# Attention and two expert layers on one core: half splits begun later, one weight chunk in four of the first layer whole, logits on strips, a new border

## The chip, the cores and the metric

One core of a Trainium2 chip runs the whole program. Its engines work side by side, each in its own fixed order, and meet by semaphores: TensorE (PE; its weight loads are listed apart as PEld), VectorE (DVE), ScalarE (ACT), GpSimd (POOL) and SyncE (SP, which here only issues DMAs). The metric is the device time of one execution in microseconds (us).

## The reference

Causal linear attention with a decay per head, then two layers of experts with top-1 routing, in float32:

```python
for t in range(768):                         # 2 batches, 8 heads of 64
    state = gamma * state + outer(k[t], v[t])
    y[t] = (q[t] @ state) / 8
x = y as 1536 tokens x 512
# layer A: tokens with x @ w_skip > 0, 8 experts, hidden size 1024
e = argmax(x @ w_gate); g = softmax weight of e
x = x + g * (relu(x @ w1[e]) @ w2[e])        # the other tokens stay as they are
# layer B: every token, other weights, at most 384 tokens for an expert
out = g' * (relu(x @ w1'[e']) @ w2'[e'])
```

Each layer has 8 experts of 2 x 512 x 1024 weights: 32 chunks of 128 x 2048 float32 (1 MB), so 64 chunks in all.

## The kernel before

**Attention** goes over 6 chunks of 128 positions with 2 batches each (`attention`). For a chunk, `scores` multiplies q and k, `state` adds k·v into the running state (k is first scaled by the decays on POOL, `scale_k`), `outs` forms the output. The kernel is written as generators; after each `yield` one step of the side work is taken (`step_side`), and the order so written is each engine's order. Side work of a chunk is `sink` in `route_tokens`: router logits, choice of the expert (`pick`, some seven small DVE operations), the token's rank among its expert's tokens (`ranked`), its place as a row of ones and zeros (`where`), and `to_slots`, which adds the token's number into a table of slots on PE. Rows go to a table in DRAM, from which each expert's 128 tokens are gathered. The **border** is the last chunk's sink: the first expert's tokens are put together on PE without the table (`place`).

**Layer A** takes the experts in turn: `layer1` (24 matmuls of 512 columns), a transposed hidden block (`split_T`), and one expert later `layer2` (24 matmuls). A float32 product is made of three fast ones (`mm3`): each weight chunk is split into a high part `hi` (ACT copy, L197) and a low part `lo` (DVE subtraction, L198), activations likewise. After each part of such work a *turn* takes place: one step of the routing into layer B (`route_b`: row, transposes, logits, choice, rank, `whereb`, `to_slots`) and, every second turn, `pump`, which splits one whole chunk and issues one load. Raw chunks land in 3 tiles during attention and 4 afterwards, split chunks live in 4 and then 6 pairs of tiles. An expert has 11 turns: four in `layer1`, one for the next x, four in `layer2`, two for the hidden block's transposes.

**Layer B** runs expert 0's first half on 128 tokens, then the other half, then the experts 1 to 7 on 256 tokens each (`pair_layer1`, `pair_layer2`, 8 turns for an expert).

At the start POOL's order holds all constants (`constants`, L132 to L148), which wait for a DMA of constants, and then the first `scale_k`. SP issues the loads of chunk 1 ahead of the DMA of those constants.

Of the kernel before, what the change touches and what calls it, by code (L numbers as in the profile page):

```python
# [26 lines left out]
NRAW, NRAW2 = 3, 1  # L27
NW, NW2 = 4, 2
# [12 lines left out]
def kernel(  # L41
# [54 lines left out]
    row2 = [const.tile([128, RW], F32, name=f"row2{i}") for i in range(3)]  # L96
# [6 lines left out]

    mask = const.tile([128, 2, 4, 128], F32, name="mask")
    row0 = const.tile([128, 2, 128], F32, name="row0")
    gq = cs[:, C_GQ:C_GQ + 512].rearrange("p (r t) -> p r t", r=4)
    rev = cs[:, C_REV:C_REV + 8]
    zsum = const.tile([128, 8], F32, name="zsum")
# [17 lines left out]
    def constants():  # L126
# [3 lines left out]
        nc.sync.dma_start(out=table[0:1, :], in_=zb[0:1, :].bitcast(F32))  # L130
        for t in t9.values():
            nc.gpsimd.memset(t, 0.5)  # L132
        nc.gpsimd.memset(cum, 0.0)
        nc.gpsimd.memset(cumb, 2.0)
        for t in row2:
            nc.gpsimd.memset(t[:, DM:RW], 0.0)
# [7 lines left out]
        nc.gpsimd.tensor_tensor(out=zsum, in0=ident[:, 8:16], in1=ident[:, 40:48], op=ALU.add)  # L144
        for i in (72, 104):
            nc.gpsimd.tensor_tensor(out=zsum, in0=zsum, in1=ident[:, i:i + 8], op=ALU.add)
# [10 lines left out]
    def add_chunks(ap, e, kind):  # L157
        for j in range(2):
            order.append(((kind, e, j), ap[e, j]))
# [11 lines left out]
    raw_free, w_free = [raw_p] * NRAW, [w_p] * NW  # L171
    count = {"load": 0, "split": 0}
    held = {}

    def load_w():
        i = count["load"]
        if i < len(order) and raw_free:
            count["load"] += 1
            pool = raw_free.pop(0)
            t = pool.tile([128, 2048], F32, tag="raw", name="raw")  # L180
            nc.sync.dma_start(out=t, in_=order[i][1])
            raw_t[i] = (t, pool)

    def split_w(n=1):

        i = count["split"]
        count["split"] += 1
        key = order[i][0]
        pool = w_free.pop(0)
# [3 lines left out]
        raw, raw_pool = raw_t.pop(i)  # L193
        r3 = raw.rearrange("p (k f) -> p k f", k=4)
        parts = [slice(4 * j // n, 4 * (j + 1) // n) for j in range(n)]
        for j, k in enumerate(parts):
# [16 lines left out]
    def first_splits():  # L213
        while w_free and count["split"] < len(order):
            while count["split"] >= count["load"]:
                yield
            yield from split_w(4)
            yield
            load_w()
# [100 lines left out]
    def route_tokens(rows, rows_p):  # L320

        late, acc, xhl, m_of = [], [], [], {}

        def sink(c, xt, bs, psum):
            rc = rows[c % len(rows)]
            end = c == NCH - 1
            n = len(bs)
            b0, b1 = bs[0], bs[-1] + 1
            lt = psum("s", 4)
            for i, b in enumerate(bs):  # L330
                for k in range(KT):
                    nc.tensor.matmul(
                        out=lt[:, 32 * i:32 * i + 18], lhsT=xt[:, b, k, :], rhs=wgt[:, k, 0:18],
                        start=k == 0, stop=k == KT - 1, skip_group_check=True,
                    )
            nc.gpsimd.tensor_copy(out=rc[:, b0:b1, IDCOL:IDCOL + 1], in_=tok[:, b0:b1, c:c + 1])
            yield
            lg = lt[:, 0:32 * n].rearrange("p (a c) -> p a c", a=n)
            m, gate = pick(lg, n, 2, None, rc[:, b0:b1, GCOL:GCOL + 2])
            m3 = m.rearrange("p (a g) j -> p a (g j)", a=n)  # L340
            m2d = m.rearrange("p n j -> p (n j)")
            rhs = sm.tile([128, n, 2, 16], BF16, tag=f"rhs{n}", name="rhs")
            eng = nc.vector if end else nc.gpsimd
            if not end:
                gate()
            if end and not acc:
                acc.extend([psum("m"), psum("m")])
                place(acc, a0, ident, True, False)
                for w in late[0:2]:
                    place(acc, *w, False, False)  # L350
            yield
            xrs = []

            def rows_T(b):
                xr = psum("s", 4)
                for k in range(KT):
                    nc.tensor.transpose(xr[:, 128 * k:128 * k + 128], xt[:, b, k, :], ident)
                nc.scalar.activation(out=rc[:, b, 0:DM], in_=xr, func=ACTF.Copy)

            def rank():  # L360
                rk = psum("s", 4)
                ranked(rk, lc[:, 0, :], m2d, cum[:, 0:n, :].rearrange("p a j -> p (a j)"), [m_of[0]] if end and b0 else [])
                pr = sm.tile([128, n, 16], F32, tag=f"pr{n}", name="pr")
                sl = sm.tile([128, n], F32, tag=f"sl{n}", name="sl")
                rk3 = rk[:, 0:16 * n].rearrange("p (a j) -> p a j", a=n)
                nc.vector.tensor_tensor(out=pr, in0=rk3, in1=m3, op=ALU.mult)
# [22 lines left out]
            if not end:  # L389
                for b in bs:  # L390
                    rows_T(b)
                    yield
# [729 lines left out]
```

## Time and profile before

| | |
|---|---|
| median of 3 runs | 488.28 us (485.61 to 489.3) |
| the profiled execution's own time | 484.47 us |
| its span (first to last instruction) | 482.7 us |
| PE busy | 407.8 us, 84% of the span |
| PEld, DVE, ACT, POOL busy | 71%, 53%, 43%, 28% |
| mean granted clock of TensorE | 0.927 of 2.4 GHz |
| moved by DMA | 96.24 MB, 199 GB/s over the span |

The share of busy time is a mean over stages with different limits, so the stages are read apart: attention with its border (to 102.45 us), layer A's expert 0 (to 109.86), its experts 1 to 7 (to 259.74), the passage to layer B with the last product of A and the first of B (to 298.32), and layer B. A row names line, engine, operation, written tile <- read tiles, shape and count; a matmul's own time runs to its modelled end, so how fast matmuls follow each other is read from two starts. A plain float32 matmul stands as two instructions in the trace.

### The profile page before, as it was taken

Reading aid. Unit: us, or ns where it says so; the run is one execution under the profiler, and the core shown is the slowest. Engines: PE = TensorE matmul, PEld = TensorE weight load, DVE = VectorE, ACT = ScalarE, POOL = GpSimd, SP = SyncE. Lnnn points to the kernel's source line nnn. Section 1 sums busy time; section 2 is a strip of 40 time slices with the busy share of each in tenths; the row PEclk is TensorE's granted clock in tenths of the full one; section 3 lists DMA queues with packets and bytes.
Section 4 is the critical chain, followed back from the end, with each engine's and each line's share of the span. In section 5 each row is a group of like instructions: output and inputs, shape, how many; then the busy total and the mean of one; then the engine's idle time right before and its main releaser. Section 6 shows DMA issues by size and latency. Waiting matters only on the chain. (4 is left out here: it accounts for less than half of the span.)

```text
span 482.7 us, 6907 instructions
## 1 busy us (share of the span) xinstructions
PE 407.8 (84%) x2734; PEld 342.6 (71%) x2734; DVE 253.8 (53%) x404; ACT 209.5 (43%) x260; POOL 135.3 (28%) x188
## 2 busy tenths in 40 slices
PE   7498888978488776967776779899999999999994
PEld 3377777967456564755555557798989898989993
DVE  4055854559646746655585341675546464646110
ACT  0235523158463553744362320755555454545111
POOL 2456744158020403121013105011413132232201
PEclk9599989899888997979796889999999999999999
DMA  8477894159945847474756344385857575631100
GB/s 329 168 303 292 321 338 168 45 200 328 366 175 195 310 170 236 179 261 134 238 188 234 109 154 134 100 286 178 281 177 276 177 258 182 239 125 45 43 1 33
DMA packets 17979, 96.24 MB, mean 199 GB/s; under 512 B 2447, under 2 KB 2575, under 8 KB 8340
## 3 DMA queue, kind: packets, MB, share of 16 engines
q1 hardware_dynamic: 11636, 80.06, 47.2%
q0 software_dynamic: 3360, 10.02, 6.0%
q10 hardware_dynamic: 2944, 5.65, 3.2%
q8 instruction: 23, 0.38, 0.3%
q14 instruction: 16, 0.13, 0.1%
HBM read 87.29 MB, written 9.48 MB: 200 GB/s over the span
## 5 line engine op out<-in xcount | busy, mean ns | idle before, releaser
L198 DVE TENSOR_TENSOR lo<-raw,hi 128x2048 fp32r<-128x2048 f32 (+1 forms) x76 | 149.8, 1980 | 109.3 <-ACT hi L197 109.3
L197 ACT ACTIVATE hi<-raw 128x2048 fp32r<-128x2048 f32 (+1 forms) x76 | 123.6, 1640 | 40.3 <-issue 19.8
L641 PE MATMUL o<-hi,hTh 128*128 128x512 f32 x192 | 84.0, 438 | 1.4 <-ACT hTh L313 1.4
L643 PE MATMUL o<-hi,hTl 128*128 128x512 f32 x192 | 81.0, 422 | 2.4 <-DVE hTl L314 2.4
L642 PE MATMUL o<-lo,hTh 128*128 128x512 f32 x192 | 80.5, 419 | 0.0
L641 PE MATMUL s<-xh,hi 128*128 128x256 f32 x224 | 63.7, 284 | 0.0
L643 PE MATMUL s<-xh,lo 128*128 128x256 f32 x224 | 63.4, 283 | 0.0
L642 PE MATMUL s<-xl,hi 128*128 128x256 f32 x224 | 63.4, 283 | 0.0
L749 POOL DMA_INDIRECT out_dram<-y,ixo x16 | 18.1, 1131 | 135.0 <-ACT y L746 103.2
L643 PEld LDWEIGHTS o<-hi,hTl 128*128 128x128 f32 x192 | 39.5, 206 | 12.3 <-DVE hTl L314 3.2
L641 PEld LDWEIGHTS o<-hi,hTh 128*128 128x128 f32 x192 | 39.2, 204 | 9.0 <-ACT hTh L313 1.6
L642 PEld LDWEIGHTS o<-lo,hTh 128*128 128x128 f32 x192 | 39.6, 206 | 7.3
L641 PEld LDWEIGHTS s<-xh,hi 128*128 128x128 f32 x224 | 42.9, 192 | 0.3
L642 PEld LDWEIGHTS s<-xl,hi 128*128 128x128 f32 x224 | 42.9, 192 | 0.3
L643 PEld LDWEIGHTS s<-xh,lo 128*128 128x128 f32 x224 | 42.9, 192 | 0.0
L641 PE MATMUL s<-hi,xh 128*128 128x512 f32 x80 | 35.6, 445 | 1.9 <-DVE xl L314 0.9
L716 POOL TENSOR_SCALAR rhsb<-m,cs 128x8 bf16<-128x8 bf16 x8 | 2.5, 309 | 123.0 <-DVE se L255 123.0
L887 ACT ACTIVATE hTh<-s 128x512 fp32r<-128x512 f32 x28 | 16.8, 599 | 41.6 <-PE s L643 41.6
L888 DVE SCALAR_TENSOR_TENSOR hTl<-s,hTh 128x512 fp32r<-128x512 f32 x28 | 19.3, 689 | 28.3 <-ACT hTh L887 28.3
L643 PE MATMUL s<-hi,xl 128*128 128x512 f32 x80 | 32.4, 406 | 0.9 <-DVE xl L314 0.9
L642 PE MATMUL s<-lo,xh 128*128 128x512 f32 x80 | 32.5, 406 | 0.0
L515 DVE TENSOR_TENSOR p<-s,mask 128x512 f32<-128x512 f32 x24 | 15.4, 685 | 26.9 <-PE s L506 26.9
(155 smaller groups left out, 566.5 us busy)
## 6 DMA issues: line engine op xcount, KB each, us to landing
raw<-in_w1a_dram SPq DMA_DIRECT2D x16, 1024.0 KB, 5.6
raw<-in_w2a_dram SPq DMA_DIRECT2D x16, 1024.0 KB, 6.8
raw<-in_w1b_dram SPq DMA_DIRECT2D x16, 1024.0 KB, 5.1
raw<-in_w2b_dram SPq DMA_DIRECT2D x16, 1024.0 KB, 5.0
kv<-in_qkv_dram SPq DMA_DIRECT2D x6, 1024.0 KB, 9.9
qk<-in_qkv_dram SPq DMA_DIRECT2D x5, 1024.0 KB, 7.7
table<-rowc ACTq DMA_DIRECT2D x5, 516.0 KB, 4.1
table<-row ACTq DMA_DIRECT2D x8, 258.0 KB, 3.3
```

The lines of the kernel that those rows point to most:

```text
L197: nc.scalar.activation(out=hi[:, k], in_=r3[:, k], func=ACTF.Copy)
L198: nc.vector.tensor_tensor(out=lo[:, k], in0=r3[:, k], in1=hi[:, k].bitcast(F32), op=ALU.subtract)
L515: nc.vector.tensor_tensor(out=t.rearrange("p r t -> p (r t)"), in0=sa[j], in1=mask[:, j].rearrange("p r t -> p (r t)"), op=ALU.mult)
L641: nc.tensor.matmul(out=acc, lhsT=a[0], rhs=w[0], start=first, stop=False)
L642: nc.tensor.matmul(out=acc, lhsT=a[0], rhs=w[1], start=False, stop=False)
L643: nc.tensor.matmul(out=acc, lhsT=a[1], rhs=w[0], start=False, stop=last)
L716: nc.gpsimd.tensor_scalar(out=rhs[:, 0, :], in0=m, scalar1=p1, scalar2=None, op0=ALU.mult)
L749: new = nc.gpsimd.indirect_dma_start(out=out[:, :], out_offset=bass.IndirectOffsetOnAxis(ap=ix, axis=0), in_=y, in_offset=None, bounds_che ...
L887: nc.scalar.activation(out=hi[:, g:g + 2, :], in_=acc, func=ACTF.Relu)
L888: nc.vector.scalar_tensor_tensor(out=lo[:, g:g + 2, :], in0=acc, scalar=0.0, in1=hi[:, g:g + 2, :].bitcast(F32), op0=ALU.max, op1=ALU.subtract
```

## The change

- **Splits in halves.** `pump` runs at every turn and issues half a chunk's split (n = 2; in attention still a quarter, n = 4, from chunk 2 on). A chunk may be split only four turns after its load was issued (`LANDING`), and a pair of tiles is given out only two turns after its last use. Raw tiles are 3 and then 5, pairs 4 and then 5. In layer B's experts 1 to 7 a turn issues two halves.
- **Whole chunks.** The second `w2a` chunk of each of the 8 experts of layer A is not split: `layer2` multiplies it as float32 out of its raw tile, against a hidden half that is only copied.
- **Logits on strips.** In attention the four partial products of the router stand in four strips of 32 columns and are added up by a second matmul after an ACT copy, where 48 matmuls with 18 columns stood.
- **Border and start.** `to_slots` of the chunks comes a step later; the last chunk's sink is written out by itself; the small DMAs of constants are issued ahead of chunk 1's loads and the constants are worked out after the first `scale_k`. `route_b` puts one more turn between `whereb` and `to_slots`.

```diff
-NRAW, NRAW2 = 3, 1
-NW, NW2 = 4, 2
+LANDING = 4
+NRAW, NRAW2 = 3, 2
+NW, NW2 = 4, 1
...
+    def whole(kind, j):
+        return kind == "w2a" and j == 1
...
     def load_w():
-        i = count["load"]
-        if i < len(order) and raw_free:
+        while count["load"] < len(order) and raw_free:
+            i = count["load"]
...
+            key, _, divided = order[i]
+            if divided:
+                raw_t[i] = (t, pool, count["turn"])
+            else:
+                wt[key], held[key] = t.rearrange("p (k f) -> p k f", k=4), pool
+
+    def next_split():
+        while count["split"] < len(order) and not order[count["split"]][2]:
+            count["split"] += 1
+        i = count["split"]
+        if i in raw_t and w_free and w_free[0][0] <= count["turn"] and raw_t[i][2] + LANDING <= count["turn"]:
+            return i
...
     def used(key):
-        w_free.append(held.pop(key))
-
-    def pump():
-        if w_free and count["split"] < count["load"]:
-            for _ in split_w():
-                pass
-        load_w()
+        pool = held.pop(key)
+        if key in whole_keys:
+            raw_free.append(pool)
+        else:
+            w_free.append((count["turn"] + 2, pool))
...
+    def pump(n, pieces):
+        count["turn"] += 1
+        for _ in range(pieces):
+            if not splitting:
+                i = next_split()
+                if i is None:
+                    break
+                splitting.append(split_w(i, n))
+            try:
+                next(splitting[0])
+            except StopIteration:
+                splitting.clear()
+        load_w()
...
+        def logits(xt, bs, psum):
+            n = len(bs)
+            ls = psum("s", 4)
+            for k in range(KT):
+                nc.tensor.matmul(
+                    out=ls[32 * k:32 * k + 32, 0:128 * n], lhsT=wgt[:, k, :], rhs=xt[:, bs[0]:bs[-1] + 1, k, :], start=True, stop=True
+                )
+            lgs = sm.tile([128, 256], F32, tag="lgs", name="lgs")
+            nc.scalar.activation(out=lgs[:, 0:128 * n], in_=ls[:, 0:128 * n], func=ACTF.Copy)
+            return lgs
+
+        def summed(lgs, n, psum):
+            lt = psum("s", 4)
+            for i in range(n):
+                nc.tensor.matmul(
+                    out=lt[:, 32 * i:32 * i + 18], lhsT=lgs[:, 128 * i:128 * i + 128], rhs=zsum[:, 0:18], start=True, stop=True
+                )
+            return lt[:, 0:32 * n].rearrange("p (a c) -> p a c", a=n)
...
+        def last_chunk(xt, psum):
...
+            lg[0] = logits(xt, [0], psum)
+            yield
+            picked(0)
+            rows_T(xt, rc, 0, psum)
+            yield
+            lg[1] = logits(xt, [1], psum)
+            warm(psum("m"), 2)
+            picked(1)
+            placed(0)
+            rows_T(xt, rc, 1, psum)
+            acc = [psum("m"), psum("m")]
+            place(acc, a0, ident, True, False)
+            placed(1)
+            to_slots(where[0], rhs[0][:, 0], 0, 16)
+            place(acc, *late[0], False, False)
+            for b in range(B):
+                gates[b]()
+                write_rows(nc.scalar, rc[:, b:b + 1, :], 1)
...
+            for g in range(2):
+                ks = slice(2 * g, 2 * g + 2)
+                place(acc, *late[1], False, True, range(KT)[ks])
+                split(acc[g][:, 0:256].rearrange("p (k t) -> p k t", k=2), hi[:, ks], lo[:, ks])
...
-                    if c + 1 < NCH:
-                        load(c + 1)
-                    if pump and c == 0:
-                        constants()
...
+                if pump and c == 0:
+                    constants()
+                if c + 1 < NCH:
+                    load(c + 1)
+                if pump and c:
+                    load_w()
+                if c < NCH - 1:
+                    scale_k(c)
+                if pump and c == 0:
+                    derived()
...
     def layer2(hT, kind, e):
...
+            if whole(kind, k // 4):
+                nc.tensor.matmul(out=acc, lhsT=a[0][:, k % 4, :], rhs=w[:, k % 4, :], start=k == 0, stop=k == FT - 1)
+            else:
+                mm3(acc, at_k(a, k % 4), at_k(w, k % 4), k == 0, k == FT - 1)
...
             late.append((r2, oh))
-        yield
+        yield from idle(2)
         to_slots(where, rhs, 8, 8)
...
-        turns[0] += 1
-        if turns[0] % 2:
-            pump()
+        pump(2, pieces[0])
```

The order moves most on POOL at the start. Before, from the first constant that reads the DMA of constants (`cs`) to the second chunk's `scale_k`:

```order
L138 MEMSET rowc_103 128x2x4
L139 ISA
L139 TENSOR_SCALAR his<-cs 128x12
L141 TENSOR_SCALAR iota<-cs 128x128 x2
L144 TENSOR_TENSOR zsum<-cs 128x8
L146 TENSOR_TENSOR zsum<-zsum,cs 128x8 x2
L147 CAST lc<-cs 128x256
L148 CAST cap<-cap_i 1x1
L483 TENSOR_TENSOR kv<-kv,cs 128x512 x2
L497 TENSOR_TENSOR gqc<-cs 128x512
```

And in the changed program, on POOL from the row mask on:

```order
L516 MEMSET row_133 1x128 x2
L549 ISA
L549 TENSOR_TENSOR kv<-kv,cs 128x512 x2
L132 MEMSET t_108 128x9
L132 MEMSET t_109 128x18
...
L137 TENSOR_SCALAR his<-cs 128x12
L139 TENSOR_SCALAR iota<-cs 128x128 x2
L142 TENSOR_TENSOR zsum<-cs 128x32
L144 TENSOR_TENSOR zsum<-zsum,cs 128x32 x2
L145 CAST lc<-cs 128x256
L146 CAST cap<-cap_i 1x1
L563 TENSOR_TENSOR gqc<-cs 128x512
```

The scaling of k (`kv`) now stands ahead of everything that reads the second DMA of constants.

DVE in one expert of layer A before, from the end of the choice (`RECIPROCAL`) to the next hidden block (`lo` is a weight split, `xl` the next x, `prb` to `whereb` the rank, `row` the token rows, `hTl` the hidden block):

```order
L258 RECIPROCAL row_97<-sf 128x1
L198 TENSOR_TENSOR lo<-raw,hi 128x2048
L314 TENSOR_TENSOR xl<-t,xh 128x512
L198 TENSOR_TENSOR lo<-raw,hi 128x2048
L722 TENSOR_TENSOR prb<-t,m 128x8
L724 TENSOR_REDUCE slb<-prb 128x1
L726 TENSOR_SCALAR whereb<-iota,slb 128x256
L198 TENSOR_TENSOR lo<-raw,hi 128x2048 x2
L686 SCALAR_TENSOR_TENSOR row_98<-o,rowc_103 128x512
L314 TENSOR_TENSOR hTl<-t,hTh 128x512 x2
```

The same stretch of DVE in the changed program:

```order
L279 RECIPROCAL row_1213<-sf 128x1
L212 TENSOR_TENSOR lo<-raw,hi 128x1024 x2
L335 TENSOR_TENSOR xl<-t,xh 128x512
L212 TENSOR_TENSOR lo<-raw,hi 128x1024
L802 TENSOR_TENSOR prb<-t,m 128x8
L804 TENSOR_REDUCE slb<-prb 128x1
L806 TENSOR_SCALAR whereb<-iota,slb 128x256
L212 TENSOR_TENSOR lo<-raw,hi 128x1024 x3
L766 SCALAR_TENSOR_TENSOR row_1214<-o,rowc_100 128x512
L335 TENSOR_TENSOR hTl<-t,hTh 128x4x128
```

Three halves stand ahead of the rank where two whole splits stood, three more halves ahead of `row` where two whole ones stood, and one of the two `hTl` is gone.

PE around `to_slots` (L278, L299) in the same expert, changed program (`hTw` is the hidden half that is only copied):

```order
L717 MATMUL o<-lo,hTh 128x512
L718 MATMUL o<-hi,hTl 128x512
L743 MATMUL o<-raw,hTw 128x512 x2
L299 LDWEIGHTS whereb
L299 MATMUL tab<-rhsb,whereb 128x8
...
L299 LDWEIGHTS whereb
L299 MATMUL tab<-rhsb,whereb 128x8
L743 MATMUL o<-raw,hTw 128x512 x2
L699 MATMUL t<-cs,h 128x128 x8
```

Before, six fast matmuls stood between the rank's matmuls and `to_slots`; now these six and two plain float32 ones do.

## Rows read from the trace of the kernel before

**Rows 1.** Windows: span, PE, PEld, DVE, ACT, POOL busy; clock, DMA share, GB/s.
```profile
109.86:259.74 149.88, 115.00 (x540) 87.12 (x540) 94.31 (x125) 77.05 (x82) 34.71 (x47) 0.86 0.67 235
259.74:298.32 38.58, 28.37 (x148) 21.48 (x147) 15.32 (x37) 10.43 (x17) 7.53 (x15) 0.87 0.39 128
298.32:476.50 178.18, 175.96 (x1120) 159.70 (x1120) 89.08 (x80) 84.28 (x88) 39.76 (x41) 1.00 0.49 164
151.59:161.86 10.27, 10.27 (x59) 7.71 (x57) 7.21 (x14) 8.27 (x11) 2.85 (x4) 1.00 0.53 186
```
**Rows 2.** Waits: who waited for whom, us in total, times, longest.
```profile
PE tab L278 <- DVE whereb L726: 21.6, 6, 3.8
PE t L700 <- DVE row L686: 16.4, 4, 6.1
PE u L528 <- POOL kv L483: 8.3, 1, 8.3
PE tab L278 <- DVE where L380: 7.2, 6, 2.5
```
**Rows 3.** Timeline, POOL and PE: start, us, operation, idle before.
```profile
15.41 0.33 POOL L139 TENSOR_SCALAR his<-cs 128x12 f32<-128x12 f32 x1 [11.50 <-DMA cs<-in_cst_dram]
17.94 2.03 POOL L483 TENSOR_TENSOR kv<-kv,cs 128x512 f32<-128x512 f32 x2
22.79 1.49 PE L506 MATMUL s<-qk 64*128 64x128 f32 x16
```
**Rows 4.** Window of the start, columns as in 1.
```profile
5.20:5.70 0.50, 0.50 (x3) 0.16 (x2) 0.00 (x0) 0.00 (x0) 0.00 (x0) 1.00 1.08 422
```
**Rows 5.** Timeline of PE: a chunk's logits; strips in layer A.
```profile
38.35 1.96 PE L332 MATMUL s<-wgt,xt 128*128 128x18 f32 x16
154.99 0.43 PE L706 MATMUL t<-x2t,wgt 128*32 128x128 f32 x8
155.34 0.50 PE L641 MATMUL s<-hi,xh 128*128 128x512 f32 x1
156.86 0.28 PE L711 MATMUL t<-zsum,lgsb 128*128 128x8 f32 x2
```
**Rows 6.** Window of the border, columns as in 1.
```profile
88.81:102.45 13.64, 10.14 (x87) 9.65 (x86) 7.46 (x41) 2.91 (x7) 0.87 (x1) 0.87 0.18 68
```
**Rows 7.** Timeline of DVE, border: a choice's first and last step.
```profile
90.75 0.17 DVE L238 TENSOR_REDUCE mx<-s 128x2 f32<-128x16 f32 x1 [0.66 <-PE s L332]
91.73 0.18 DVE L251 TENSOR_TENSOR m<-t,tm 128x16 bf16<-128x16 f32 x1
```
**Rows 8.** Timeline of DVE, layer A: the rank and the place.
```profile
164.66 0.15 DVE L722 TENSOR_TENSOR prb<-t,m 128x8 f32<-128x8 f32 x1
165.04 0.35 DVE L726 TENSOR_SCALAR whereb<-iota,slb 128x256 bf16<-128x256 f32 x1
```
**Rows 9.** Groups by line: busy us, mean ns of one, idle before.
```profile
L198 DVE TENSOR_TENSOR lo<-raw,hi 128x2048 fp32r<-128x2048 f32 x60 | 137.3, 2291 | 103.7 <-ACT hi L197 103.7
L198 DVE TENSOR_TENSOR lo<-raw,hi 128x512 fp32r<-128x512 f32 x16 | 12.5, 813 | 5.6 <-ACT hi L197 5.6
L314 DVE TENSOR_TENSOR xl<-t,xh 128x512 fp32r<-128x512 f32 x23 | 15.1, 684 | 7.4 <-issue 7.4
L686 DVE SCALAR_TENSOR_TENSOR row<-o,rowc 128x512 f32<-128x512 f32 x8 | 6.0, 747 | 9.6 <-PE o L643 9.6
```
**Rows 10.** Timeline of PE: plain float32 matmuls, and what follows.
```profile
7.14 1.02 PE L454 MATMUL s<-cs,row 128*128 128x512 f32 x2
8.00 0.38 PE L460 MATMUL u<-zb 128*128 128x512 bf16 x1
```
**Rows 11.** Timeline of PE: layer A's first product, both ends.
```profile
102.45 0.50 PE L641 MATMUL s<-hi,xh 128*128 128x512 f32 x1 [0.93 <-DVE xl L314]
...
108.04 0.60 PE L634 MATMUL t<-cs,h 128*128 128x128 f32 x4
```
**Rows 12.** DMA issues: tile, count, KB each, us from issue to landing.
```profile
raw<-in_w1a_dram SPq DMA_DIRECT2D x16, 1024.0 KB, 5.6
```

More of the change, by code (lines that the diff above doesn't have):

```diff
@@ L405, in sink, with counted, slots_of @@
-            yield
-            for i in range(n):
-                to_slots(where[:, i, :], rhs[:, i], 0, 16)
-            if c == NCH - 3:
+            return rhs
+        def counted(m):
+            nc.gpsimd.tensor_tensor(out=cum, in0=cum, in1=m.unsqueeze(1).to_broadcast([128, 2, 16]), op=ALU.add)
+        def slots_of(sl, i):
+            where = rows_p.tile([128, 256], BF16, tag="where", name="where", bufs=4)
+            nc.vector.tensor_scalar(out=where, in0=iota, scalar1=sl[:, i:i + 1], scalar2=None, op0=ALU.is_equal)
+            return where
@@ new lines, in sink @@
+        def sink(c, xt, psum):
+            if c == NCH - 1:
+                yield from last_chunk(xt, psum)
+                return
+            rc = rows[c % len(rows)]
+            bs = list(range(B))
+            lgs = logits(xt, bs, psum)
+            nc.gpsimd.tensor_copy(out=rc[:, :, IDCOL:IDCOL + 1], in_=tok[:, :, c:c + 1])
+            yield
+            lg = summed(lgs, B, psum)
+            m, gate = pick(lg, B, 2, None, rc[:, :, GCOL:GCOL + 2])
+            m3 = m.rearrange("p (a g) j -> p a (g j)", a=B)
+            gate()
+            rhs = numbers(nc.gpsimd, m3, c, bs)
+            yield
+            rows_T(xt, rc, 0, psum)
+            yield
+            rows_T(xt, rc, 1, psum)
+            yield
+            rk = psum("s", 4)
+            ranked(rk, lc[:, 0, :], m.rearrange("p n j -> p (n j)"), cum.rearrange("p a j -> p (a j)"))
+            sl = slot(rk, m3, B)
+            where = [slots_of(sl, i) for i in bs]
+            write_rows(nc.scalar, rc, B)
+            for i in bs:
+                counted(m3[:, i, :])
+            yield
+            if c < NCH - 2:
+                yield
+            for i in bs:
+                to_slots(where[i], rhs[:, i], 0, 16)
+            if c == NCH - 2:
@@ L602 @@
+        for _ in scores(0, 0):
+            pass
+        for c, b in units:
+            for _ in main(c, b):
+                step_side(c, b)
+        for g in side:
+            for _ in g:
+                pass
+    attention(a_p, psa, first, route_tokens(rowc, a_p), pump)
     at.close()
@@ L775 @@
     side = []
-    turns = [0]
+    pieces = [1]
     def step_side():
@@ L795, in run @@
             step_side()
-    for _ in range(NRAW2):
-        load_w()
+    load_w()
     hT = {}
@@ L920 @@
     emit_out(xs2[0, 1], acc)
+    pieces[0] = 2
     for e in range(1, E):
```

293 lines of the change are left out of this document (121 added, 172 removed).

## The prediction

> **What bounds the kernel now.** I read the windows by stage first, since the mean shares hide that the stages have different limits. In layer B PE is busy 175.96 of 178.18 us at clock 1.00 [rows 1]: nothing but PE counts there, and the change leaves PE's order there alone. Layer A's experts 1 to 7 take 149.88 us, 21.4 each, with PE busy only 115.00 of it at a mean clock of 0.86, and no other engine is full. The passage to layer B (38.58 us) looks alike: PE busy 28.37 at 0.87. So there PE waits, and after a long wait also runs below full speed.
>
> The list of waits says for what [rows 2]. In layer A `to_slots` waits 6 times for `whereb` (21.6 us) and the transposes of the token rows 4 times for `row` (16.4 us, up to 6.1 at once). At the start PE waits 8.3 us for the scaled k; in attention `to_slots` waits for `where` (7.2). All wait for DVE or POOL, and none is long to compute: the rank up to `whereb` takes 165.04 + 0.35 − 164.66 = 0.73 us [rows 8], `row` 0.75 [rows 9]. What makes them late stands ahead of them in DVE's order: two whole weight splits of 2.29 us, where a split itself waits for ACT's copy (103.7 us of idle time) [rows 9]. The profiled execution took 484.47 us, 3.8 under the median of 488.28. The sum is made against it and then taken from the median.
>
> **a) Start, −7.5 us.** POOL's `his` waits until 15.41 for the second DMA of constants, and the scaling of k behind it starts at 17.94 though it doesn't need them [rows 3]. These constants were issued behind chunk 1's loads, two of 1024 KB. Those and the constants are 2.4 MB; at the 422 GB/s of the early window [rows 4] 5.7 us, so chunk 0's kv has landed by 15.4 − 5.7 = 9.7. The scaling's first half takes 2.03 / 2 = 1.0, so the state starts near 10.8 instead of 19.0. From the state to the second chunk's scores lie 22.79 − 19.0 = 3.8 us; that would give 14.6. Chunk 1's loads now go behind four small DMAs, so I take 15.3: −7.5. Bounds: −8.2 (these DMAs cost nothing) and +2.5 (the start is gained, then lost on chunk 1's later loads). The Trainium skill ("SBUF — State Buffer", section "A bandwidth-pool intuition that's wrong (but worth ruling out)") gives HBM to one core about 358 GB/s and calls it almost always the bottleneck; by it the 2.4 MB take 6.7 us, chunk 1 is whole 1.0 later, and this term would be −6.5. The window with 422 speaks against it here.
>
> **b) Logits on strips, −3.** A chunk's logits hold PE 1.96 us [rows 5]. The same sums on strips exist in layer A: eight half instructions of 128 columns from 154.99 to 155.34, so 0.35 for one batch, and the adding-up 0.28 [rows 5]. For two batches that is 0.70 + 0.4 = 1.1: −0.84 for each of 6 chunks, −5. But an ACT copy now stands between the two, and the choice starts later; I give back 2. Bounds −5 and +1 (copy uncovered in every chunk). The Trainium skill ("TensorE: Matmul & The Clock Gate", section "Measured speedup vs the span model") lets packed strips cost about one matmul plus 4 ns for each further one; by that the four take 0.43 for two batches instead of 0.70, and the term would be some 1.6 larger. The row of layer A decides.
>
> **c) `to_slots` a step later in attention, −2.6.** Of the 7.2 us, about 4.6 lie in the chunks before the border. Some 0.65 us of score matmuls now stand ahead of each of them. Bounds −4.6 and 0.
>
> **d) Border, −4.5.** From the last output to layer A's first matmul pass 13.64 us, PE busy 10.14 at 0.87 [rows 6], because both batches' logits, choices and ranks go through one after the other. Written out, the chain for the last batch is: copy of x 0.69 (as long as `xl` [rows 9]), strips 0.35, ACT copy 0.4 (an estimate between the 0.17 of a small operation and 0.69), adding-up 0.28, choice 91.91 − 90.75 = 1.16 [rows 7], rank and place 0.73 + 0.35 [rows 8], product with the place and the split into hi and lo in two halves, some 3: 7.0, and eight handovers between engines of about 0.25: 9. Bounds −7 and 0 (the waits only move).
>
> **e) Layer A, experts 1 to 7, −39.3.** PE alone first. The window 151.59:161.86 has no wait, full clock, all 24 matmuls of `layer1`, half of `layer2` and the routing: 10.27 us [rows 1]. The other half of `layer2` is now plain float32. Two half instructions take 8.00 − 7.14 = 0.86 [rows 10]; three fast ones take 3 × 0.233 = 0.70, from 24 in 108.04 − 102.45 [rows 11]. So four cost 3.44 instead of 2.8: +0.65 for each expert. With the transposes of the hidden block, 0.60 [rows 11], and about 0.4 for `to_slots` and the token rows' transposes, PE alone takes 14.7 us. A second way agrees: 115.00 × 0.86 / 7 = 14.1, and 0.65 are 14.8.
>
> Then DVE. A half's subtraction lies between 2291 / 2 = 1.15 and the line through 813 ns for 512 and 2291 for 2048, 1.31 [rows 9]; I take 1.22, as a half moves half the data and pays a start of its own. From the adding-up to the end of the choice on DVE are 1.8 us (the 1.16 and the handovers around it). Then come 3 × 1.22 + 0.68 (`xl`) + 0.73 and some handovers of ACT: `whereb` is there 7.5 us after the adding-up. PE reaches `to_slots` later than before, by two float32 products: 161.86 − 156.86 + 1.72 = 6.7 [rows 1, 5]. A wait of 0.8 stays where 3.6 stood. Three more halves and `row` are 4.4 behind `whereb`, at 11.96; PE wants it at about 11.7: 0.25. Together 14.7 + 0.8 + 0.25 = 15.8, and 7 × 15.8 = 110.6 against 149.9. The clock I take as 1.00: it was that in the window without waits, and waits of a microsecond are left. One split in four is gone from DVE and ACT; they were busy 94.31 and 77.05 of 149.88, 13.5 and 11.0 for an expert, and DVE loses 9.2 − 6 × 1.22 = 1.8 and one hidden subtraction (0.68): 11 of 15.8, so it isn't the bound. Bounds: −47 (no wait left, 14.7) and −20 (18.5, first rival).
>
> **f) Passage, −10.5.** PE busy 28.37 × 0.87 = 24.7 at full clock, +0.65 for the last float32 products, +2 for the last expert's place, behind which no other work stands, and +0.6 for what else waits: 28. Bounds −13 and −3.
>
> **Layer B, 0.** 1120 matmuls as before; a split is ready eight turns ahead of its use, and DVE and ACT are half busy. If splits came late, this cover would be gone; nothing in the rows bounds that closely, since the raw tiles even grow.
>
> Sum: −7.5 − 3 − 2.6 − 4.5 − 39.3 − 10.5 = −67.4: 417.1 for the profiled execution, **421** against the median.
>
> **Rivals.** *1. Layer A is paced by the DMAs.* They are busy 0.67 of 21.4 us [rows 1], 14.3 us for an expert; in 15.8 us that is 0.91. Loads that take 5.6 us [rows 12] may then take longer than the four turns (5.8 us) they are given, ACT's copy waits, and `whereb` behind it. With 18.5 us for an expert, halfway to before: +19, **440**. For it speaks that share; against it that 14.3 is still under 15.8. Chance 0.18.
>
> *2. Attention gains nothing until the border.* The earlier start is lost on chunk 1 and later qk, kv and weight loads, and the ACT copy eats the strips' gain. Of a to c (13.1) some 4 stay: +9, **430**. Chance 0.12. The Trainium skill's 358 GB/s would bring it nearer.
>
> *3. Slower: too few raw tiles.* A whole chunk holds its raw tile until `layer2` has used it, some 25 turns, a divided one about 6. Five tiles over 11 turns are 55 tile-turns for an expert, 25 + 3 × 6 = 43 of them used. If landings take so long that a divided chunk needs over 10 turns, loads are issued late and ACT stands at a copy whose data isn't there, with the hidden block's copies queued behind it. It decides where it costs more than 67 / 21 = 3.2 us for each of the 21 divided chunks, landings of about 9 us against 5.6 [rows 12]. With 13 us for an expert, 7 × 13 = 91: 421 + 91 = 512. Chance 0.03.
>
> *4. The change doesn't do what it says.* Halves still wait for ACT and stand ahead of `whereb`, so its wait stays and only start and border gain: 488 − 12 = **476**. Chance 0.05.
>
> **How the numbers follow.** The forecast gets 0.62. With its terms' bounds it reaches from 404 (c to f near their better ends) to 436. Taking in rivals 1 and 2, the range is 404 to 446; left out are rivals 3 and 4 and the tails, under 2 in 10. About 1% is what a measurement of this kernel can tell from no change. Faster: 0.62 + 0.18 + 0.12 and most of rival 4, 0.95; within 1%: 0.02; slower: 0.03.
>
> **What would show it.** The first state matmul near 11 and the second chunk's scores near 15 (a); strips of two batches within 0.7 us (b); 9 us from the last output to layer A's first matmul (d); 15.8 us between the same matmuls of two experts, waits for `whereb` and `row` under 1 us, a granted clock near 1.00, two float32 half instructions 0.86 apart (e); layer B still 178 us. Wrong I would be if ACT's copies wait for DMAs in layer A, if the clock stays below 0.9 there, or if `whereb` keeps waits of 3 us.

## The result, and the profile after

The changed kernel takes **427.28 us** (424.64 to 428.95, 4 runs) beside 486.94 of the kernel before on the same chip: ratio 0.877, 95% interval 0.870 to 0.884. The forecast was 421 in a range of 404 to 446. The profiled span went from 482.7 to 424.7 us, −58.0, where the sum said −67.4. Medians here and below take in every execution, while the ratios leave out those over 1.5% above the fastest of their kernel, among them one of 1294 us in experiment 3 and one of 2092 us in experiment 7, of which no trace tells the cause.

By stage, from the starts and ends of the same instructions in both traces:

| stage | before | after | difference | predicted |
|---|---|---|---|---|
| attention, to the last output (a, b, c) | 88.82 | 77.06 | −11.8 | −13.1 |
| border (d) | 13.64 | 12.35 | −1.3 | −4.5 |
| first product of expert 0 to that of expert 1 | 7.41 | 10.85 | **+3.4** | none |
| experts 1 to 7 of layer A (e) | 149.88 | 108.65 | −41.2 | −39.3 |
| passage (f) | 38.58 | 28.52 | −10.1 | −10.5 |
| layer B, to the end | 184.4 | 187.3 | **+2.9** | 0 |

The windows of the changed kernel that answer to [rows 1] and [rows 6] (border; four experts between the adding-up of their logits; passage; layer B):

```profile
77.06:89.41 12.35, 8.38 (x76) 6.82 (x75) 6.48 (x34) 3.13 (x9) 2.44 (x6) 0.86 0.28 97
119.31:179.49 60.18, 59.39 (x305) 40.70 (x304) 42.67 (x80) 37.40 (x56) 16.70 (x27) 1.00 0.85 310
208.91:237.43 28.52, 25.24 (x144) 17.97 (x143) 10.84 (x36) 7.68 (x16) 9.59 (x18) 1.00 0.65 235
237.43:424.70 187.27, 178.18 (x1120) 159.73 (x1120) 92.76 (x108) 87.92 (x116) 33.01 (x43) 0.99 0.46 158
```

Four experts now take 60.18 us, 15.05 each, with PE busy 59.39 of it at clock 1.00: layer A is bound by PE. Its DMAs are busy 0.85 of the time and keep up. The waits of PE, beside [rows 2]:

```profile
PE t L780 <- DVE row L766: 4.2, 2, 2.7
PE tab L299 <- DVE where L392: 4.1, 4, 1.2
PE s L572 <- DMA qk<-in_qkv_dram: 3.3, 2, 3.0
PE t L699 <- DMA rowc<-table,ids: 2.9, 1, 2.9
PE m L328 <- DMA a<-table,ids: 2.7, 1, 2.7
PE t L699 <- DVE hTl L335: 2.2, 1, 2.2
PE tab L299 <- DVE whereb L806: 1.1, 6, 0.2
```

`whereb` fell from 21.6 us to 1.1, `row` from 16.4 to 4.2. Three waits at the top are for DMAs. Two of them, for the gathered tokens `a` and `rowc`, the kernel before did not have; the third, for a qk load, rose from 1.9 us, and the wait for the hidden half `hTl`, which stands in layer B, from 1.4. Before:

```profile
PE s L506 <- DMA qk<-in_qkv_dram: 1.9, 1, 1.9
PE t L634 <- DVE hTl L314: 1.4, 1, 1.4
```

At the start (POOL, then PE; beside [rows 3] and [rows 5]):

```profile
9.54 2.04 POOL L549 TENSOR_TENSOR kv<-kv,cs 128x512 f32<-128x512 f32 x2 [6.24 <-DMA kv<-in_qkv_dram]
...
10.64 0.69 PE L594 MATMUL u<-kv 128*64 128x64 f32 x16
...
13.13 1.16 PE L572 MATMUL s<-qk 64*128 64x128 f32 x16
...
16.43 0.64 PE L347 MATMUL s<-xt,wgt 128*32 128x256 f32 x8 [0.46 <-ACT xt L628]
17.00 0.72 PE L572 MATMUL s<-qk 64*128 64x128 f32 x8
```

The scaling waits for its kv alone, which lands at 9.5, and the state starts at 10.64 (forecast 10.8). The second chunk's scores start at 13.13 (forecast 15.3). A chunk's strips take 17.00 − 16.43 = 0.57 us (forecast 0.70).

### The profile page after: what moved, and what is told of

Read it like the earlier page. It is cut to its first block, busy times and chain, and to the rows that moved or that the text cites. A ratio compares the mean times of both kernels' runs of the same rounds, so it can differ in the third digit from the quotient of the medians.

```text
span 424.7 us, 6847 instructions
## 1 busy us (share of the span) xinstructions
PE 391.5 (92%) x2672; PEld 315.6 (74%) x2672; DVE 239.0 (56%) x431; ACT 202.1 (48%) x311; POOL 118.9 (28%) x191
## 5 line engine op out<-in xcount | busy, mean ns | idle before, releaser
L212 DVE TENSOR_TENSOR lo<-raw,hi 128x1024 fp32r<-128x1024 f32 (+1 forms) x120 | 139.3, 1194 | 61.0 <-ACT hi L211 59.9
L211 ACT ACTIVATE hi<-raw 128x1024 fp32r<-128x1024 f32 (+1 forms) x120 | 113.8, 997 | 4.5 <-DMA raw<-in_w1b_dram 4.2
L716 PE MATMUL o<-hi,hTh 128*128 128x512 f32 x160 | 65.5, 409 | 0.2 <-ACT hTh L334 0.2
L718 PE MATMUL o<-hi,hTl 128*128 128x512 f32 x160 | 63.6, 398 | 0.8 <-DVE hTl L335 0.8
L717 PE MATMUL o<-lo,hTh 128*128 128x512 f32 x160 | 63.4, 396 | 0.0
L718 PEld LDWEIGHTS o<-hi,hTl 128*128 128x128 f32 x160 | 30.1, 188 | 8.8 <-DVE hTl L335 1.7
L964 ACT ACTIVATE hTh<-s 128x512 fp32r<-128x512 f32 x28 | 16.7, 598 | 40.2 <-PE s L718 39.9
L716 PEld LDWEIGHTS o<-hi,hTh 128*128 128x128 f32 x160 | 30.1, 188 | 6.5 <-ACT hTh L334 0.5
L717 PEld LDWEIGHTS o<-lo,hTh 128*128 128x128 f32 x160 | 30.2, 189 | 6.2
L826 ACT ACTIVATE y<-o,rowc 128x512 f32<-128x512 f32 x15 | 10.3, 688 | 47.5 <-issue 29.5
L743 PE MATMUL o<-raw,hTw 128*128 128x512 f32 x64 | 30.6, 603 | 0.0
```

The source lines that it names most:

```text
L211: nc.scalar.activation(out=hi[:, k], in_=r3[:, k], func=ACTF.Copy)
L212: nc.vector.tensor_tensor(out=lo[:, k], in0=r3[:, k], in1=hi[:, k].bitcast(F32), op=ALU.subtract)
L716: nc.tensor.matmul(out=acc, lhsT=a[0], rhs=w[0], start=first, stop=False)
L717: nc.tensor.matmul(out=acc, lhsT=a[0], rhs=w[1], start=False, stop=False)
L718: nc.tensor.matmul(out=acc, lhsT=a[1], rhs=w[0], start=False, stop=last)
L743: nc.tensor.matmul(out=acc, lhsT=a[0][:, k % 4, :], rhs=w[:, k % 4, :], start=k == 0, stop=k == FT - 1)
```

## Experiments

Ratios are to the kernel before on the same chip, with the 95% interval; the changed kernel had 0.877 (0.870 to 0.884) and, repeated, 0.883 (0.878 to 0.889). Differences in time from the changed kernel are worked out from the ratios, against both of these, since not all runs were on one chip. The end of attention is told where it matters, since it moves by itself: in the nine profiled executions whose order of work is the same up to there (the changed kernel twice, and experiments 1, 2, 3, 5, 6, 9 and 12) it lies between 75.8 and 81.2 us, in six of them at 77.1 or less. It goes with the granted clock up to there: 0.95 to 0.96 where attention ends at 75.8 to 76.6, 0.93 at 77.1, 0.91 at 79.7 and 80.1, 0.89 at 81.2. The two ends of this row are the repeated changed kernel and experiment 5:

```profile
0.00:75.75 75.75, 64.51 (x789) 51.46 (x790) 48.02 (x120) 31.50 (x68) 43.73 (x75) 0.95 0.79 304
0.00:81.22 81.22, 69.06 (x790) 54.47 (x790) 49.53 (x120) 31.50 (x68) 41.60 (x75) 0.89 0.75 284
```

### 1. Whole splits again in layer A: 0.923 (0.917 to 0.930)

```diff
-        pump(2, pieces[0])
+        pump(1, 1 if count["turn"] % 2 else 0) if pieces[0] == 1 else pump(2, pieces[0])
```

> Changed kernel, but in layer A and the passage a chunk is split whole again, at every second turn (all else stays: landing distance, whole chunk per expert, to_slots one turn later). Theory A (what counts is how much DVE has ahead of whereb and row): two whole splits of 2.3 us stand ahead of whereb in every second expert and one in the others, where three halves stood; whereb comes some 0.9 us later in three experts and no row comes later, so PE waits grow by 1 to 3 us in all: 0 to +5 us. Rival B (the size of a piece itself counts: the subtraction begins only after the whole copy, and small operations queue behind 2.3 us): waits of 2 to 3 us per expert come back and the clock falls with them: +15 to +30 us.

449.15 us, by the ratios 19 to 22 us more than the changed kernel: rival B by the size. The single waits for `whereb` are below rival B's 2 to 3 us, though, and the clock stays at 1.00 in the middle experts; what adds up stands in more places than either saw. DVE and PE of one expert, the one split of DVE ahead of `whereb` in the next, and then PE's wait for `whereb` in total and the window of four experts:

```profile
140.06 2.29 DVE L212 TENSOR_TENSOR lo<-raw,hi 128x2048 fp32r<-128x2048 f32 x1 [0.95 <-ACT hi L211]
142.27 0.68 DVE L335 TENSOR_TENSOR xl<-t,xh 128x512 fp32r<-128x512 f32 x1
142.87 2.30 DVE L212 TENSOR_TENSOR lo<-raw,hi 128x2048 fp32r<-128x2048 f32 x1
145.09 0.15 DVE L802 TENSOR_TENSOR prb<-t,m 128x8 f32<-128x8 f32 x1
...
145.89 0.26 PE L299 MATMUL tab<-rhsb,whereb 128*128 128x8 bf16 x4 [1.70 <-DVE whereb L806]
...
158.10 2.29 DVE L212 TENSOR_TENSOR lo<-raw,hi 128x2048 fp32r<-128x2048 f32 x1 [2.42 <-ACT hi L211]
```

```profile
PE tab L299 <- DVE whereb L806: 8.0, 6, 1.7
120.50:187.10 66.60, 59.82 (x305) 40.57 (x304) 41.77 (x68) 36.34 (x44) 19.36 (x27) 1.00 0.80 293
```

Where two splits stand ahead of `whereb`, PE waits 1.70; where one stands, 0.97, because that one waits 2.42 us for ACT's copy of the whole chunk. With 0.7 for `row` in every second expert an expert takes 16.65 us instead of 15.05. Four longer waits at single places (4.4 us for a gather, 4.4 and 2.3 for `row`, 4.1 for the first hidden block of layer B) make up most of the rest, and stretches at clock 0.5 begin in or just behind each of these four. So the halves themselves are worth about a third of the whole gain: 19 to 22 of 60 us.

### 2. No whole chunk: 0.878 (0.872 to 0.884)

```diff
-        return kind == "w2a" and j == 1
+        return False
...
-        turn = split_T(h, FT, "hT", (True, False))
+        turn = split_T(h, FT, "hT")
```

> Changed kernel, but no chunk is used whole as float32: all 32 chunks of layer A are split in halves. Theory A (PE bounds an expert now, 15.05 us apart in the changed profile; the order of DVE keeps three halves ahead of whereb and six ahead of row): PE saves 0.65 us per expert, the two more halves of DVE and ACT find room: -3 to -5 us. Rival B (the split work or the landings of raw chunks are what the whole chunk relieves): an expert takes 17 us or more, waits for whereb or row of over 1 us each: +10 us or more.

Neither: the time is the same. Four experts of it, with the columns as above:

```profile
126.90:186.97 60.07, 57.81 (x322) 43.41 (x322) 54.17 (x92) 44.57 (x64) 16.73 (x27) 1.00 0.89 311
```

PE is busy 1.6 us less in four experts, and waits 0.5 instead of 0.2 us for `whereb` in each; DVE is busy 54.2 of 60.1 instead of 42.7. The float32 chunk takes DVE work away, and costs PE what that saves. The whole time hides more than this, though: in this profile the sixth expert, which takes 19.4 us in the changed kernel, takes 15.0, while attention ends at 79.7 and PE waits 5.4 us for the second expert's gathered tokens instead of 2.9.

### 3. `to_slots` one turn earlier: 0.903 (0.894 to 0.913)

```diff
-        yield from idle(2)
+        yield
```

> Changed kernel, but to_slots of layer A comes one turn earlier again (before the first two of the four float32 products instead of between them). Theory A: whereb ends about 0.2 us after PE gets there now; two float32 products (1.72 us) fewer ahead of it make PE wait about 1.9 us for whereb in each of six experts: +8 to +13 us, if the clock stays. Rival B: the waits are long enough to halve the granted clock after each: +20 us or more. Rival C (the wait is only moved, what follows was waiting as long): 0 to +3 us.

441.73 us, by the ratios 10 to 13 us more than the changed kernel: theory A. PE waits 1.9 us for `whereb` six times, as the sum said, and an expert takes 16.7 us:

```profile
PE tab L299 <- DVE whereb L806: 11.5, 6, 1.9
```

### 4. Six turns from a load to its split: 0.878 (0.870 to 0.885)

```diff
-LANDING = 4
+LANDING = 6
```

> Changed kernel with six turns instead of four from a load to its split. The order of DVE in layer A changes at one place only: in the sixth expert one half instead of three stands ahead of row, where the changed profile shows PE waiting 2.73 us for row. Theory A (that wait comes from a first chunk of layer B that ACT takes up before it has landed, 4.2 us of idle time of ACT): the wait goes, with the half clock behind it: -3 to -4 us. Rival B (row waits for something else there): the wait stays, 0. Attention's splits move a step or two, which should cost under 1 us.

In the changed kernel the sixth expert shows this on ACT and DVE:

```profile
189.43 2.00 ACT L211 ACTIVATE hi<-raw 128x1024 fp32r<-128x1024 f32 x2 [4.22 <-DMA raw<-in_w1b_dram]
...
190.53 2.36 DVE L212 TENSOR_TENSOR lo<-raw,hi 128x1024 fp32r<-128x1024 f32 x2 [2.90 <-ACT hi L211]
192.80 0.74 DVE L766 SCALAR_TENSOR_TENSOR row<-o,rowc 128x512 f32<-128x512 f32 x1
```

With six turns that wait is gone, and the sixth expert takes 15.0 us instead of 19.4: theory A, −4.4. The total didn't move, because the wait for the second expert's gathered tokens became 7.72 us instead of 2.87. In that run, and then in the changed kernel, SP's loads and POOL's gather:

```profile
PE t L699 <- DMA rowc<-table,ids: 7.7, 1, 7.7
87.53 0.33 SPq L184 DMA_DIRECT2D raw<-in_w1a_dram  x1
...
94.80 2.15 POOL L318 DMA_INDIRECT rowc<-table,ids  x1 [11.80 <-ACT hi L211]
```

```profile
86.53 1.47 ACTq L311 DMA_DIRECT2D table<-rowc  x2
...
88.70 0.33 SPq L184 DMA_DIRECT2D raw<-in_w1a_dram  x1
...
91.10 1.10 POOL L318 DMA_INDIRECT rowc<-table,ids  x1 [8.66 <-DMA table<-rowc]
```

The gather can't start before the border's last rows have been written to the table (258 KB each, issued last at 87.34 and 86.98). Two weight loads of 1024 KB follow the write by 0.2 us there, where it takes 6.6 us from issue to landing, and by 1.7 here, where the gather is issued 4.1 us behind it.

### 5. `to_slots` ahead of the border's last product: 0.885 (0.881 to 0.889)

```diff
+            to_slots(where[1], rhs[1][:, 0], 0, 16)
+            nc.vector.tensor_copy(out=ids, in_=tab)
             for g in range(2):
...
             x0.append((hi, lo))
-            to_slots(where[1], rhs[1][:, 0], 0, 16)
-            nc.vector.tensor_copy(out=ids, in_=tab)
```

> Changed kernel, but the last to_slots of the border and the cast of the numbers stand ahead of the last product that puts the first expert's tokens together, as they stood before the change. Theory A (the new wait of 2.87 us for the second expert's gathered tokens comes from the table of slots being read some 3 us later against layer A's first product): the gather is issued 1 to 2.5 us earlier, the wait shrinks to 0.5 to 1.5 us and with it the half clock behind it: -2 to -4 us, less 0.3 us for four small matmuls in the border's chain. Rival B (the gather waits for the rows written to the table, not for the numbers): wait stays, 0 to +0.5.

Rival B: the wait is 2.57 us, and the gather is issued 2.1 us after layer A's first matmul, no earlier than in the changed kernel (1.7), though the numbers (`ids`) are there 3.9 us before it:

```profile
91.45 0.17 DVE L477 CAST ids<-tab 128x24 int32<-128x24 f32 x1
...
95.47 1.10 POOL L318 DMA_INDIRECT rowc<-table,ids  x1 [8.98 <-DVE lo L212]
```

The time itself, 429.38, shows no cost of the edit: its interval overlaps both of the changed kernel's, and attention ended at 81.2 in the profiled execution.

### 6. `a0` behind the last rank: 0.876 (0.871 to 0.881)

```diff
-            place(acc, a0, ident, True, False)
             placed(1)
             to_slots(where[0], rhs[0][:, 0], 0, 16)
-            place(acc, *late[0], False, False)
+            place(acc, *late[0], True, False)
+            place(acc, a0, ident, False, False)
```

> Changed kernel, but the product with the first gathered block (a0) stands behind the last batch's rank and the first batch's own product instead of ahead of them. Theory A (the border took 12.35 us and not 9 because PE stands 2.73 us at that product for the gather's landing, and the last rank stands behind it): the rank goes ahead, the wait is used, border 9.5 to 10.5 us: -2 to -3 us. Rival B (the gather lands as late and everything then waits for it at its new place): wait of about 2 us there, -0.5 to 0.

In the changed kernel's border PE stands at `a0` and the last rank (L285) behind it; in the run the rank goes ahead and nothing waits over 0.9 us:

```profile
83.65 1.16 PE L328 MATMUL m<-cs,a 128*128 128x128 f32 x8 [2.73 <-DMA a<-table,ids]
84.64 0.17 PE L285 MATMUL s<-m,lc 128*128 128x16 bf16 x1
```

```profile
80.87 0.18 PE L285 MATMUL s<-m,lc 128*128 128x16 bf16 x1 [0.75 <-DVE m L272]
...
82.90 1.06 PE L328 MATMUL m<-cs,a 128*128 128x128 f32 x8
...
85.78 0.50 PE L716 MATMUL s<-hi,xh 128*128 128x512 f32 x1 [0.85 <-DVE xl L335]
```

The border takes 85.78 − 76.27 = 9.51 us instead of 12.35, as theory A says, but not all of that is the edit: the granted clock was 1.00 here and 0.86 there. At clock 1.00 the old order took 11.26 us (experiment 4); at 0.85 the new one took 11.27 and 11.15 (experiments 10 and 12):

```profile
77.72:88.98 11.26, 6.70 (x74) 5.26 (x76) 6.38 (x34) 3.09 (x9) 2.62 (x6) 1.00 0.29 95
80.85:92.12 11.27, 8.34 (x75) 6.83 (x75) 6.40 (x34) 3.13 (x9) 2.40 (x6) 0.85 0.31 106
```

So at a like clock the edit is worth 1.1 to 1.8 us, less than theory A's 2 to 3. In the times it doesn't stand clear of the interval.

### 7. The old start: 0.901 (0.897 to 0.906)

```diff
+                if c + 1 < NCH:
+                    load(c + 1)
                 if pump and c == 0:
                     constants()
-                if c + 1 < NCH:
-                    load(c + 1)
+                    derived()
...
-                if pump and c == 0:
-                    derived()
```

> Changed kernel with the old start: chunk 1's loads ahead of the small DMAs of constants, and the constants ahead of the first scaling of k. Theory A: the state starts near 19 again instead of 10.6 and attention ends later by it: +6 to +8.4 us. Rival B (attention is bound by its DMAs, which run on meanwhile: in the changed profile one wait for a qk load, 3.0 us, stands at 53.6): a part is caught up, +2 to +5 us.

439.51 us, by the ratios 9 to 12 us more than the changed kernel. The state starts at 19.02 again, and attention ends at 87.5, outside everything seen with the new start:

```profile
19.02 1.12 PE L594 MATMUL u<-kv 128*64 128x64 f32 x16 [8.02 <-POOL kv L549]
13.80:23.90 10.10, 4.88 (x58) 4.48 (x60) 0.00 (x0) 2.61 (x5) 5.54 (x11) 0.50 0.34 133
```

Theory A, and more than it. A stretch of 10 us at clock 0.5 begins in PE's wait of 8.02 us and outlasts it by 5. How much is caught up behind it can't be told, since attention's end lies 6 to 12 us later than in the executions with the new start.

### 8. No strips: 0.879 (0.874 to 0.883)

```diff
-            ls = psum("s", 4)
-            for k in range(KT):
-                nc.tensor.matmul(
-                    out=ls[32 * k:32 * k + 32, 0:128 * n], lhsT=wgt[:, k, :], rhs=xt[:, bs[0]:bs[-1] + 1, k, :], start=True, stop=True
-                )
...
-            nc.scalar.activation(out=lgs[:, 0:128 * n], in_=ls[:, 0:128 * n], func=ACTF.Copy)
-            return lgs
+            return xt, bs
...
+            for i, b in enumerate(lgs[1]):
+                for k in range(KT):
+                    nc.tensor.matmul(
+                        out=lt[:, 32 * i:32 * i + 18], lhsT=lgs[0][:, b, k, :], rhs=wgt[:, k, 0:18], start=k == 0, stop=k == KT - 1
+                    )
```

> Changed kernel, but attention's logits are 48 matmuls of 18 columns straight into one tile again, at the place where now the strips are added up, with no copy by ACT. Theory A (the strips saved about 0.5 us of PE in each chunk net of the copy): +2 to +5 us. Rival B (PE waits for DMA or DVE in attention and border anyway): 0 to +1. Rival C (the copy by ACT costs as much as the strips save): 0 or a little less.

Inconclusive: 427.52 us, and attention ends at 79.0, inside the spread of the changed kernel's order. At a like clock up to there (0.94, in the changed kernel 0.93) PE is busy 69.58 us instead of 66.96 and attention ends 1.9 us later, a hint at theory A's lower end from one execution; the times show B, C or a gain of 2 us alike.

### 9 to 11. Later loads, three edits together, and the changed kernel again

The two loads at the border two turns later, issued by ACT (9); these, `a0` later and six turns (10); no edit (11):

```diff
+    hold = [0, 0]
...
+        if count["turn"] < hold[0]:
+            return
...
-            nc.sync.dma_start(out=t, in_=order[i][1])
+            eng = nc.scalar if hold[0] and count["load"] <= hold[1] else nc.sync
+            eng.dma_start(out=t, in_=order[i][1])
...
-    load_w()
+    hold[:] = [count["turn"] + 2, count["load"] + 2]
     hT = {}
```

> Changed kernel, but the two weight loads that were issued right behind the border's last table writes are issued two turns later, by ACT behind the first copy of the hidden block (some 4 to 5 us later, after the second expert's gather). Theory A (the wait of 2.87 us for that gather, 1.3 to 7.7 us in the runs so far, comes from these 2 MB: the sooner they follow the 258 KB table write, the later it lands): the write lands within 2.5 us, the gather within 5.5, the wait is under 0.5 us, from layer A's first product to the second expert's 7.5 to 8.5 us instead of 10.85: -2.5 to -3.5 us. Rival B (the gather is late because it is issued late): wait of 2 to 3 us stays, 0. A split of the second expert that comes too late would show as a new wait of PE for hi or lo.

> Changed kernel with three edits together: a0's product behind the last rank, the two loads behind the gather, six turns from a load to its split. From their own runs: border 9.5 us instead of 12.35, second expert's product 7.5 to 8.5 us after the first instead of 10.85, no wait of 2.7 us for row in the sixth expert (-4.4): -9 to -10.5 us of the changed kernel's 427, so 416 to 419, if none of them brings a later wait forward; 421 to 424 if one does.

> The changed kernel once more, unaltered, beside the two others on the same chip: 426 to 428 us, 0.877 of the kernel before. Its profile shows how far attention's end (77.06 us) and the gather's wait (2.87) move from one execution to the next by themselves: by up to 3 us, if the differences between the other runs' attention, whose code is the same there, are chance.

9: 433.48 us, 0.891 (0.886 to 0.897), 4 to 7 us more than the changed kernel, where 2.5 to 3.5 less were expected. The gather is issued 1.8 us after layer A's first matmul, as in the changed kernel, and PE no longer waits for it, so the loads do hold it up. But from layer A's first product to the second expert's it is still 9.95 us, 1.26 of them a wait for ACT's copy, and what the loads bring is then late, as the expectation feared: ACT waits for weights, and PE for `row` behind their splits.

```profile
114.98 2.00 ACT L215 ACTIVATE hi<-raw 128x1024 fp32r<-128x1024 f32 x2 [0.53 <-DMA raw<-in_w1a_dram]
...
119.16 0.66 PE L784 MATMUL t<-cs,row 128*128 128x128 f32 x4 [3.38 <-DVE row L770]
```

10: 424.95, 0.873 (0.868 to 0.878), a part of what was expected. In its profile the wait for the gather and the one in the sixth expert are gone, but the border takes 11.27 us and not 9.5, PE waits 2.2 us for `row` in the first expert, and attention ends at 80.9.

11: 429.85, 0.883, above the 426 to 428 expected; attention ends at 75.8, and the wait for the gather is 1.44 us instead of 2.87, with the same code. Over all runs that wait goes roughly with the loads' distance behind the last table write: 7.7 and 5.2 us at 0.2, 5.4 and 2.6 at 0.9, 1.3 to 4.4 at 1.3 to 1.8, 1.4 at 3.0, none at 6.8 and 7.4; before the change, with one load 3.2 us behind, none.

### 12. Two edits: 0.8665 (0.861 to 0.872)

```diff
+    landing = [LANDING]
...
-        if i in raw_t and w_free and w_free[0][0] <= count["turn"] and raw_t[i][2] + LANDING <= count["turn"]:
+        if i in raw_t and w_free and w_free[0][0] <= count["turn"] and raw_t[i][2] + landing[0] <= count["turn"]:
...
     load_w()
+    landing[0] = 6
     hT = {}
```

and the edit of 6.

> Changed kernel with two edits: a0's product behind the last rank, and six turns from a load to its split from layer A on (four in attention, so that its splits stay as they are); the weight loads as in the changed kernel. Theory A (the two waits stand in different stages and fall one by one): border 9.5 us, no wait of 2.7 to 3.2 us for row in the sixth expert; -2.8 and -4.4, 7 us under the changed kernel, ratio to the kernel before 0.862 to 0.870. Rival B (six turns make the loads at the border or the first splits of layer A late, as the longer wait for the gather in the run with six turns throughout could mean): the wait for the second expert's gather is 5 us or more again, or row waits in the first experts: -2 to -4, ratio 0.870 to 0.876.

**422.80 us**, in theory A's range, and the fastest here; its interval lies clear of the repeat's (from 0.878) and overlaps the first one's (from 0.870) by 0.002. That is 5 to 8 us under the changed kernel. From the end of the border to layer B's first wait PE runs at full clock, and the wait for `row` in the sixth expert is gone; the border, though, takes 11.15 us at clock 0.85 and not the expected 9.5:

```profile
86.42:236.00 149.58, 141.86 (x723) 99.12 (x722) 93.74 (x176) 82.64 (x124) 44.83 (x71) 1.00 0.79 288
```

## Why the prediction was right, point by point

**e, right, and so the whole.** PE waited for small results behind DVE's splits, and some 70% of the gain come from layer A's experts 1 to 7. The parts of the working held singly: a half's subtraction took 1.22 us, `whereb` came 7.0 us after the adding-up for 7.5 in the sum (experiment 3 puts the two float32 products at 1.7 to 1.9 us of wait), the clock went to 1.00 in four experts and to 0.98 over all seven. The remaining wait for `whereb` is 0.2 instead of 0.8 us, so an expert takes 15.05, not 15.8; the sixth, with 2.7 us for `row` and a stretch at half clock, takes 19.4 and gives back 4.4.

What each part of the change gives in layer A: an expert takes 16.65 us with whole splits (experiment 1) and 16.7 with the earlier `to_slots` (experiment 3). PE's waits for `whereb` in these two, 8.0 and 11.5 us, add up to 19.5 where 21.6 stood [rows 2]. The two costs added to 15.05 make 18.3 us, against 21.4 before, when the waits for `row` (16.4 us [rows 2]) and a clock of 0.86 came on top; in the experts read from 1 and 3 it was 1.00. The float32 chunk gives nothing (experiment 2). What the four turns from a load to its split and the other number of raw tiles and pairs give is not shown: no run takes them back.

Mis-sized in it: four float32 half instructions take 143.37 − 141.57 = 1.80 us, 0.45 each and not 0.43:

```profile
141.57 1.96 PE L743 MATMUL o<-raw,hTw 128*128 128x512 f32 x4
143.37 0.38 PE L699 MATMUL t<-cs,h 128*128 128x128 f32 x2
```

**Rival 1 fell.** The DMAs are busy 0.85, and PE 0.99, of four experts. Where a landing did come late (the sixth expert, shown under experiment 4), it cost one place, not every expert.

**a, right in its cause and too small.** State at 10.64 for 10.8, but the second chunk's scores start 9.7 us earlier and not 7.5, beyond the bound of 8.2. The 3.8 us that the sum puts between the two were read where the clock was 0.50; at 1.00 they are 13.13 − 10.64 = 2.5:

```profile
19.03:22.79 3.76, 3.76 (x49) 3.36 (x49) 0.00 (x0) 1.53 (x2) 1.94 (x2) 0.50 0.02 4
```

**c, next to nothing.** Of the 7.2 us of waits for `where` [rows 2], 4.6 lay in the chunks before the border, and these are still 4.1: 0.5 of the 2.6 came. **b** stays open (experiment 8). The qk wait of up to 3.0 us is a little of rival 2. That a to c together gave 11.8 of 13.1 is in part luck: more from a makes up for c.

**d, wrong as a term.** The step that failed is "written out, the chain for the last batch is": it followed the last batch's data and left out the product with `a0`, which stands ahead of that batch's rank in PE's order and waits 2.73 us for a gather. Moving it is worth 1.1 to 1.8 us at a like clock (experiment 6). The chain also counted nothing for the clock: it was 0.86 in the border, with PE busy 8.38 us, where the same order at 1.00 has 6.70 (experiment 4). The 9.51 us of experiment 6, near the forecast 9, have both out of the way.

**Not priced: +3.4 us behind the border.** I costed what the border loses, but not what is late next: the second expert's gathered tokens. PE didn't wait for them before; now it waits 2.87 us, with a stretch at half clock behind it. The last write of rows is issued 2.4 us before layer A's first product instead of 4.0, with two weight loads close behind. Experiment 5 excludes the numbers as the cause, and 9 and 4 speak for the loads.

**f, right.** 28.52 us for 28, at clock 1.00, with PE busy 25.24 of them.

**Layer B, 0 forecast, +2.9.** Its first hidden block waits 2.18 instead of 1.45 us. The other 2.2 are seven times the same thing: the second product of an expert takes longer, in the kernel before and after:

```profile
325.34:336.34 11.00, 11.00 (x52) 9.10 (x51) 6.47 (x5) 5.40 (x6) 1.05 (x1) 1.00 0.52 185
```

```profile
265.38:276.70 11.32, 11.32 (x51) 9.13 (x50) 5.46 (x7) 5.46 (x8) 1.07 (x2) 1.00 0.56 187
```

Each of its 48 matmuls follows after 234 ns instead of 227, at clock 1.00 in both. It is so in the changed kernel and in all its variants here. The code of the product is the same; the number of raw and split tiles beside it is not, but no run changes that alone. The cause stays open.

## What to carry to other kernels

When a small operation on one engine releases another, count what stands ahead of it in its engine's order, and cut that into pieces that start as soon as half of their input is there: half the grain was worth about 20 us here. Read the granted clock of a stretch before taking a length from it, and compare two borders or two attentions at a like clock only. For each step that becomes shorter, follow the next datum needed after it, to its DMA, and look what else is issued on the DMAs just then. An edit that takes work off one engine and puts as much on another, as the whole chunk does, gave nothing here, where PE was busy 59 and DVE 43 to 54 of 60 us.

## What the runs showed that I had not expected

- PE waited 2.6 to 7.7 us for a gather behind a write of 258 KB when 2 MB of loads were issued within a microsecond of the write, and not at all when they were issued some 7 us behind it.
- The same program's border ran at clock 1.00 in one execution (9.51 us, experiment 6) and at 0.85 with the same order of work in another (11.15 us, experiment 12), though PE's waits there were the same, 0.7 to 0.9 us:

```profile
76.27:85.78 9.51, 6.81 (x75) 5.17 (x75) 6.31 (x34) 3.13 (x9) 2.46 (x6) 1.00 0.35 124
```

```profile
76.50:87.65 11.15, 8.44 (x75) 6.80 (x75) 6.33 (x34) 3.13 (x9) 2.46 (x6) 0.85 0.31 107
```

- Attention's end moves by up to 5.5 us between executions with the same order of work, and goes with the granted clock up to there, from 0.96 to 0.89. What brings the clock down in one execution and not in another no run here separated.
